# Hash attention and a gated block on one core: weight pieces rounded a row later, with three staging buffers, and the late pairs' sums and hash products put between rows

## The chip, the core and the metric

The kernel runs on one core of a Trainium2 chip. The metric is the device time of one execution in microseconds. A profiled execution gives, besides its time, the span from its first to its last instruction and the granted clock of TensorE. The engines are called PE (TensorE: matmuls), PEld (PE's weight loads), DVE (VectorE), ACT (ScalarE), POOL (GpSimd, which here mainly issues DMAs) and SP (SyncE, which issues DMAs). L146 is line 146 of the kernel before.

## What is computed

The first part is attention in which a query sees only the keys of its own hash bucket; the second is a SwiGLU block on the joined heads.

```python
# q, k, v: (4, 8, 768, 64); proj: (64, 6)
q_bucket = sum((q @ proj > 0) * 2**arange(6))        # k_bucket likewise
scores = where(q_bucket == k_bucket, q @ k.T / 8, -1e9)
attn = exp(scores - max); attn = attn / (sum(attn) + 1e-9)
x = (attn @ v).transpose(0, 2, 1, 3).reshape(3072, 512)
g = x @ w_gate; val = x @ w_val                      # (512, 1536) each
out = (g * sigmoid(g) * val) @ w_out                 # (1536, 512)
```

The three weight matrices come as 64-bit floats, which the kernel reads as pairs of 32-bit words and turns into 32-bit parts itself.

## The kernel before

**Attention.** Two heads of one batch make a pair: 16 pairs, four per batch. A pair has two rows of work, one for each half of its 768 queries (`half` 0 and 1), and a row has six chunks of 128 keys. For each chunk, PE makes the scores of both heads in two PSUM banks: a product of q and k (`sc<-qT,kT`, L428) and, added to it, a product of their hash bits (`sc<-qb,kb`), which decides whether a key is seen. ACT takes the exponentials (`A<-sc`, L431). DVE adds the chunks' exponentials up for the row sums (`acc`, L459 and L463). After the six chunks of a row, PE multiplies the exponentials by v (`av`, L442), and ACT copies the result out (`xT`, L452; `e`, L451). Seven banks serve the scores, the transposes, the hash products (`hps`) and the sums (`sum`); one bank holds `av`.

**Sums.** `total(n)` has PE sum `acc` over the partitions (L474), ACT copy the result to `row` (L477), and SP send it to `few`. `invert` takes reciprocals on DVE (L483), has SP store them and load them back spread over the partitions (L492). `norm` multiplies on DVE (L498). A pair of batch 0 is then split into three parts: ACT rounds it (`high`, L201), and DVE makes the rest (L204, L208). A pair of a later batch is stored to DRAM. Before, `total(n-1)` stands in row (n, 0), after the second chunk; `invert` after that row's scores; `norm` after the scores of row (n, 1).

**The next pair.** `front(n + 1)` gives the steps that make the next pair's `qT`, `kT` and hash bits. The transposes are PE's up to pair 4; from pair 5 on (here the "late" pairs, prepared from pair 4 on) they are DVE's (L396). The last step, `hash_next`, multiplies by the hash directions on PE (L355), takes signs on ACT (L360) and copies q's bits to a second set of partitions with a DMA that SP issues (L372, `qb<-qb`). It stands in row (n, 1) after the third chunk, and the signs of k after the row's last chunk.

**Weight pieces.** The weights are cut into 36 pieces. A piece of words is loaded by POOL (`words`, L116), and `scale` prepares it on ACT with two instructions (L123 into the staging buffer, L124). The generator `prepare` then does the rest in five steps, of which `prepare_on(5)` or `prepare_on(4)` are taken at a row's end, and one after each atom of the gated block:

```python
shift    DVE  L141
or       DVE  L143
add      DVE  L146, then the rounding on ACT  L147, then the load of words 3 pieces on
subtract DVE  L150
low      DVE  L152, then the store of the staging buffer to DRAM by POOL  L154
```

`progress["kept"]` counts the pieces whose store has been issued. `scale_ahead` scales a further piece if it is less than two ahead of `kept`; it is called once or twice between a row's scores and its `av` products, and once after them. There are two staging buffers (`stage`) and four buffers of words. The last pair's result and its spread reciprocals lie in two of the words buffers (`spare`).

**Gated block.** Three parts of x and three of each weight piece give two sums per product, `a` and `n` (L584). Per batch, 12 U items each make a gate and a value (four atoms: 16 matmuls into `a`, 8 into `n`, twice), and 4 D items multiply by `w_out` (six atoms of 9 matmuls, `o`). `a`, `n` and `o` share four buffers of two banks each. ACT evicts `a` (L626), DVE subtracts `n` (L632), ACT takes SiLU (L634), DVE multiplies (L636), ACT rounds (L637), DVE makes the two other parts of `hid` (L640, L642). In the first D of a batch ACT evicts (L671) and DVE subtracts (L676); later DVE does both. `bring` has POOL load the prepared pieces back into a ring of seven buffers (L190), so that a piece has to be stored before it is brought. The order of all engines' queues is the order in which the program text issues the instructions; nothing reorders them.

Of the kernel before, what the change touches and what calls it, by code (L numbers as in the profile page):

```python
# [8 lines left out]
FP32 = mybir.dt.float32  # L9
FP32R = mybir.dt.float32r  # L10
BF16 = mybir.dt.bfloat16
I32 = mybir.dt.int32
# [7 lines left out]
def kernel(  # L20
# [43 lines left out]
    TOWARD = 1 - 2.0**-13  # L64

    konst = ctx.enter_context(tc.tile_pool(name="konst", bufs=1))
    wordp = ctx.enter_context(tc.tile_pool(name="wordp", bufs=4))
    stagep = ctx.enter_context(tc.tile_pool(name="stagep", bufs=2))
    small = ctx.enter_context(tc.tile_pool(name="small", bufs=2))
    even_x = ctx.enter_context(tc.tile_pool(name="even_x", bufs=1))  # L70
    ringp = ctx.enter_context(tc.tile_pool(name="ringp", bufs=7))
    dram = ctx.enter_context(tc.tile_pool(name="dram", bufs=1, space=bass.MemoryType.DRAM))
    ctx.enter_context(tc.manual_schedule())
# [3 lines left out]
    def r32(t):  # L77
        return t.bitcast(FP32R)

    def finish(todo):  # L80
        while todo:
            todo.pop(0)()
# [35 lines left out]
    def scale(i):  # L118
# [5 lines left out]
        nc.scalar.activation(t[:, :, 0], top, AF.Copy, scale=2.0**-13 * (1 + 2.0**-17))  # L124
        progress["scaled"] = i + 1

    def scale_ahead():
        i = progress["scaled"]
        if i < NPIECE and i < progress["kept"] + 2 and i in words:
            scale(i)  # L130

    def prepare():
        for i in range(NPIECE):
            load_words(i + 1)
            if i not in staged:
                scale(i)
            t, st = words[i], staged[i]
            lo, hi = t[:, :, 0], t[:, :, 1]
            w = st[:, 1]
            wi = w.bitcast(I32)  # L140
            nc.vector.tensor_single_scalar(wi, wi, 3, op=ALU.logical_shift_left)  # L141
            yield True
            nc.vector.scalar_tensor_tensor(out=wi, in0=hi, scalar=-(1 << 31), in1=wi,  # L143
                                           op0=ALU.bitwise_and, op1=ALU.bitwise_or)
            yield True
            nc.vector.tensor_tensor(wi, wi, lo, op=ALU.add)  # L146
            nc.scalar.activation(r32(st[:, 0]), w, AF.Copy, scale=TOWARD)  # L147
            load_words(i + 4)
            yield True
            nc.vector.tensor_tensor(r32(w), w, st[:, 0], op=ALU.subtract)  # L150
            yield True
            nc.vector.scalar_tensor_tensor(out=r32(st[:, 2]), in0=w, scalar=-STEP, in1=st[:, 0],  # L152
                                           op0=ALU.mult, op1=ALU.add)
            nc.gpsimd.dma_start(ram[i].bitcast(FP32), st)  # L154
            progress["kept"] = i + 1
            yield True

    preparing = prepare()

# [54 lines left out]
    def attention(scope):  # L214
# [113 lines left out]
        load_words(2, nc.sync)  # L328
        for name, queue in (("q", nc.sync), ("k", nc.gpsimd), ("v", nc.sync)):
            fetch(1, name, queue)  # L330
        load_words(4)

        T = {}
        bits = {}
# [74 lines left out]
        acc = {}  # L409
        av = {}  # L410
        xT = {}
        mean = {}
        waiting = []

# [19 lines left out]
        def attend(u):  # L434
            n, half, c = units[u]
            a = weights(u)
            if c == 0:
                av[n] = av_ps.tile([P, 512], FP32, tag="av", name="av")
            ps = av[n]
            width = AW if half == 0 else HQ  # L440
            for h in range(2):
                nc.tensor.matmul(ps[h * D : (h + 1) * D, 0:width], raws["v", n][:, h, c, :],  # L442
                                 a[:, h, 0:width], start=c == 0, stop=c == NCH - 1)
            if c == NCH - 1:
                if half == 0:
                    if n == len(pairs) - 1:
                        xT[n] = spare()
                    else:
                        xT[n] = xp.tile([P, S], FP32, tag="xT", name="xT")
                    mean[n] = small.tile([P, 1], FP32, tag="e", name="e")  # L450
                    nc.scalar.activation(mean[n], ps[:, HQ : HQ + 1], AF.Copy, scale=EPS)  # L451
                nc.scalar.copy(xT[n][:, half * HQ : (half + 1) * HQ], ps[:, 0:HQ])  # L452
# [29 lines left out]
        def invert(n, few):  # L482
            nc.vector.reciprocal(few, few)  # L483
            s = sums[n % 2]
            nc.sync.dma_start(s, few)
            if n == len(pairs) - 1:
                t = spare().rearrange("p (x q) -> p x q", x=2)
            else:
                t = att.tile([P, 2, HQ], FP32, tag="r", name="r")
            flat = s.rearrange("p e -> (p e)").rearrange("(h x t) -> h (x t)", h=2, t=HQ)  # L490
            for h in range(2):
                nc.sync.dma_start(t[h * D : (h + 1) * D].rearrange("p x t -> p (x t)"),  # L492
                                  flat[h : h + 1].to_broadcast([D, 2 * HQ]))
            return lambda: norm(n, t)
# [15 lines left out]
        def prepare_pair(count):  # L510
            for _ in range(count):
                if steps:
                    rest.extend(f for f in steps.pop(0)() or [] if f)
# [5 lines left out]
        for u in range(0, N, NCH):  # L519
            n, half, _ = units[u]  # L520
            more = n + 1 < len(pairs)
            for c in range(NCH):
                score(u + c)
                if u + c == 2 or more and half == 1 and c == 2:
                    prepare_pair(1)
                if half == 1 and c == 2:
                    load(n + 2, "qk")
                if c == 1 and half == 0 and n > 0:
                    total(n - 1)
                if c:  # L530
                    add(u + c)
            finish(rest)
            if half == 0 and more:
                steps = front(n + 1)
                if u:
                    prepare_pair(2)
            if half == 0:
                while waiting:
                    last.append(waiting.pop(0)())
            else:  # L540
                finish(last)
            for _ in range(1 if u else 2):
                scale_ahead()
            for c in range(NCH):
# [12 lines left out]

    left = []

    def spare():  # L560
        t = wordp.tile([P, PIECE, 2], I32, tag="words", name="words")
        return t.rearrange("p f w -> p (f w)")[:, 0:S].bitcast(FP32)

    with ExitStack() as scope:
        attention(scope)

    def gated_block(scope):
        xs = [even_x, scope.enter_context(tc.tile_pool(name="odd_x", bufs=1))]  # L570
        hidp = scope.enter_context(tc.tile_pool(name="hidp", bufs=4))
        gatep = scope.enter_context(tc.tile_pool(name="gatep", bufs=2))
        outp = scope.enter_context(tc.tile_pool(name="outp", bufs=1))
# [120 lines left out]
        for kind, n in order:  # L694
            if kind == "U":
                b, f = divmod(n, NF)
                if f == NF - NQ and b + 1 < B:
                    for pr in range(NP):
                        x = spare()
                        nc.sync.dma_start(x, kept_x[b + 1, pr])  # L700
                        splits += split(x, b + 1, pr, xs[(b + 1) % 2])
            if kind == "D" and n == B * NF // NQ - 1:
                finish(tails)
            for atom in atoms_of(kind, n):
# [7 lines left out]
                if left and count[0] in (6, 14):  # L712
                    left.append(left.pop(0)())
                    left[:] = [f for f in left if f]
                prepare_on(1)

    with ExitStack() as scope:
        gated_block(scope)
# [32 lines left out]
```

## Time and profile before

| | |
|---|---|
| median of 8 runs | 990.69 us (988.74 to 995.2) |
| the profiled execution | 989.59 us |
| its span | 987.7 us |
| granted TensorE clock, mean | 0.989 |
| PE busy | 953.2 us (97%) |
| DVE busy | 674.8 us (68%) |
| ACT busy | 471.5 us (48%) |
| POOL busy | 124.7 us (13%) |
| first gated matmul (`a`) | at 382.16 us |

The attention part lasts until about 382 us. The first gated batch, with the last pieces of weights, runs until about 490 us; after that PE hardly stands. A line of a list of waits reads: who waited, for whom, total us, how often, longest. In the order of time a line reads: start, duration, engine, line, operation, out<-in, count, and in brackets the idle time before it and what ended it.

### The profile page before, as it was taken

The page shows a single profiled execution, that of the slowest core. Times are in us where ns is not written, and L with a number is a line of the kernel's source. Part 1 is how long each engine was busy: PE and PEld are TensorE (multiplying, and loading weights), DVE is VectorE, ACT ScalarE, POOL GpSimd, SP SyncE. Part 2 cuts the span into 40 slices and gives each one's busy share as a digit, 9 for nine tenths or more (in the row PEclk, how much of TensorE's full clock was granted, in tenths as well). Part 3 has the DMA queues.
Part 4 walks back from the last instruction along what each step waited for, and adds up shares of the span by engine and source line. Part 5 has one row for each costly group of instructions (what it writes and reads, how often), then busy time and mean ns, then how long its engine had stood idle before and what let it go on. Part 6 is the DMA issues. An engine that isn't in the chain of part 4 may idle for free.

```text
span 987.7 us, 14470 instructions
## 1 busy us (share of the span) xinstructions
PE 953.2 (97%) x5413; PEld 729.7 (74%) x5413; DVE 674.8 (68%) x868; ACT 471.5 (48%) x882; POOL 124.7 (13%) x248
## 2 busy tenths in 40 slices
PE   9988899999999999999999999999999999999998
PEld 4444444444444447989999999999999999999996
DVE  4667788778878786868886446586546586546556
ACT  6877776867767675444422332322332322232221
POOL 3110011100101012221210110110110110110100
PEclk9999999999999999999999999999999999999999
DMA  6554575776868867598955854655854655754641
GB/s 181 176 158 136 154 174 145 205 182 185 207 162 205 245 236 262 174 370 346 352 194 177 329 188 144 235 192 184 323 189 156 227 188 192 255 190 162 224 160 64
DMA packets 134262, 203.22 MB, mean 206 GB/s; under 512 B 92912, under 2 KB 98512, under 8 KB 134192
## 3 DMA queue, kind: packets, MB, share of 16 engines
q0 software_dynamic: 31008, 159.79, 45.3%
q1 hardware_dynamic: 102384, 42.30, 17.3%
q8 instruction: 43, 0.70, 0.3%
q10 hardware_dynamic: 800, 0.20, 0.1%
q14 instruction: 27, 0.22, 0.1%
HBM read 162.01 MB, written 39.42 MB: 204 GB/s over the span
## 4 chain that ended last, share of the span: by engine, by line
PE 58%; DVE 1%; issue 1%; DMA 0%; ACT 0%; POOL 0%; POOLq 0%; DVEq 0%; ACTq 0%
PE a L584 27%; PE o L584 18%; PE n L584 13%; DVE o L676 0%; DVE o L673 0%; DMA ram<-stage 0%; ACT stage L123 0%; DVE words L498 0%; DVE hid L640 0%; DVE g L632 0%; DVE stage L143 0%; ACT words L124 0%; POOL words L116 0%; ACT o L671 0%; DVE stage L141 0%
## 5 line engine op out<-in xcount | busy, mean ns | idle before, releaser
L584 PE MATMUL a<-xparts,ring 128*128 128x384 f32 x1536 | 282.7, 335 | 1.9 <-ACT row L477 1.9
L584 PEld LDWEIGHTS a<-xparts,ring 128*128 128x128 f32 x1536 | 268.9, 188 | 3.9 <-ACT row L477 2.6
L584 PE MATMUL o<-ring,hid 128*128 128x512 f32 x864 | 200.4, 391 | 2.2 <-DVE o L676 2.2
L428 PE MATMUL sc<-qT,kT 64*128 64x384 f32 x768 | 176.7, 520 | 20.0 <-ACT A L431 19.8
L584 PEld LDWEIGHTS o<-ring,hid 128*128 128x128 f32 x864 | 162.4, 188 | 35.9 <-DVE o L676 2.7
L431 ACT ACTIVATE A<-sc 128x384 f32<-128x384 f32 x384 | 156.4, 507 | 8.2 <-PE sc L428 7.5
L428 PEld LDWEIGHTS sc<-qT,kT 64*128 64x128 f32 x768 | 84.0, 193 | 90.0 <-issue 46.7
L584 PE MATMUL n<-xparts,ring 128*128 128x384 f32 x768 | 148.5, 334 | 0.0
L463 DVE TENSOR_TENSOR acc<-acc,A 128x768 f32<-128x768 f32 x128 | 122.7, 958 | 25.5 <-ACT A L431 14.4
L584 PEld LDWEIGHTS n<-xparts,ring 128*128 128x128 f32 x768 | 134.5, 188 | 0.0
L442 PE MATMUL av<-A,vraw 128*64 128x386 f32 (+1 forms) x768 | 131.2, 491 | 0.0
L190 POOL DMA_DIRECT2D ring<-ram x144 | 75.9, 529 | 432.9 <-PE n L584 278.1
L632 DVE TENSOR_TENSOR v<-v,n 128x768 f32<-128x768 f32 x48 | 45.8, 954 | 106.0 <-PE n L584 105.4
L442 PEld LDWEIGHTS av<-A,vraw 128*64 128x64 f32 x768 | 52.3, 136 | 71.9 <-issue 57.9
L626 ACT ACTIVATE g<-a 128x768 f32<-128x768 f32 x48 | 38.9, 811 | 125.8 <-PE a L584 122.6
L637 ACT ACTIVATE hid<-v 128x768 fp32r<-128x768 f32 x48 | 40.7, 848 | 118.4 <-DVE v L636 118.4
L428 PE MATMUL sc<-qb,kb 64*128 64x384 bf16 x384 | 82.9, 331 | 3.9 <-DMA qb<-qb 3.3
L634 ACT ACTIVATE g<-g 128x768 f32<-128x768 f32 x48 | 40.6, 847 | 89.2 <-DVE g L632 89.2
L676 DVE TENSOR_TENSOR o<-o 128x512 f32<-128x512 f32 x96 | 65.9, 687 | 22.1 <-ACT o L671 19.6
L632 DVE TENSOR_TENSOR g<-g,n 128x768 f32<-128x768 f32 x48 | 45.6, 950 | 33.4 <-PE n L584 33.3
L154 POOL DMA_DIRECT2D ram<-stage x36 | 19.4, 540 | 360.5 <-issue 139.9
L640 DVE SCALAR_TENSOR_TENSOR hid<-hid,v 128x768 fp32r<-128x768 f32 x48 | 45.9, 957 | 26.3 <-ACT hid L637 26.3
(77 smaller groups left out, 714.9 us busy)
## 6 DMA issues: line engine op xcount, KB each, us to landing
ring<-ram POOLq DMA_DIRECT2D x144, 768.0 KB, 5.8
ram<-stage POOLq DMA_DIRECT2D x36, 768.0 KB, 5.1
vraw<-in_v_dram SPq DMA_DIRECT2D x16, 384.0 KB
words<-in_moe_w_out_dram POOLq DMA_DIRECT2D x12, 512.0 KB, 7.7
out_dram<-o SPq DMA_DIRECT2D x24, 256.0 KB
r<-sums SPq DMA_DIRECT2D x30, 192.0 KB
words<-in_moe_w_gate_dram POOLq DMA_DIRECT2D x11, 512.0 KB, 6.8
words<-in_moe_w_val_dram POOLq DMA_DIRECT2D x11, 512.0 KB, 7.8
```

The lines of the kernel that those rows point to most:

```text
L190: nc.gpsimd.dma_start(t.bitcast(FP32), ram[at].bitcast(FP32))
L428: nc.tensor.matmul(sc[h], x["k", n][rows, ks], x["q", n][rows, qs], start=start, stop=not start)
L431: nc.scalar.activation(weights(u)[:, h, 0:HQ], sc[h], AF.Exp, scale=SCALE * (OFF / 2 if n <= NP else 1.0))
L442: nc.tensor.matmul(ps[h * D : (h + 1) * D, 0:width], raws["v", n][:, h, c, :], a[:, h, 0:width], start=c == 0, stop=c == NCH - 1)
L463: nc.vector.tensor_tensor(acc[n, half], acc[n, half], a[:, :, 0:HQ], op=ALU.add)
L584: nc.tensor.matmul(ps, w, x, start=start, stop=stop)
L626: nc.scalar.activation(two(z), ops[what][2], AF.Copy, scale=STEP + 1)
L632: nc.vector.tensor_tensor(two(z), two(z), n_, op=ALU.subtract)
L634: nc.scalar.activation(z, z, AF.Silu)
L637: nc.scalar.activation(h, val, AF.Copy, scale=TOWARD / STEP)
L640: nc.vector.scalar_tensor_tensor(out=l, in0=h.bitcast(FP32), scalar=-STEP, in1=val, op0=ALU.mult, op1=ALU.add)
L676: nc.vector.tensor_tensor(accs[c], accs[c], t[:, 1], op=ALU.subtract)
```

## The change

The generator `prepare` now works on two pieces at a time: it shifts, combines and adds piece i, and then subtracts and finishes piece i - 1. The rounding is no longer issued with the addition; the piece is put on a list, and `scale_ahead` issues the rounding at its next call, before it looks whether it may scale. A piece may be scaled if it is less than three ahead of `kept`. There are three staging buffers and three buffers of words. `scale_ahead` is also called after every atom of the gated block.

`total(n-1)` moves to the start of row (n, 1), `invert` to after that row's scores, and `norm` to after the scores of row (n+1, 0); the last pair keeps the old places. From pair 4 on, the hash products stand ahead of the scores of half 1, and the signs of k after its second chunk. The last pair's result and reciprocals get a buffer of their own, which later holds parts of x (`odd_x`); the loads of x for the next batch use the three words buffers, after all pieces have been prepared.

```diff
-    wordp = ctx.enter_context(tc.tile_pool(name="wordp", bufs=4))
-    stagep = ctx.enter_context(tc.tile_pool(name="stagep", bufs=2))
+    wordp = ctx.enter_context(tc.tile_pool(name="wordp", bufs=3))
+    stagep = ctx.enter_context(tc.tile_pool(name="stagep", bufs=3))
+    odd_x = {NP - 1: ctx.enter_context(tc.tile_pool(name="odd_x", bufs=1))}
...
+    unrounded = []
+
+    def round_up():
+        st = staged[unrounded.pop(0)]
+        nc.scalar.activation(r32(st[:, 0]), st[:, 1], AF.Copy, scale=TOWARD)
+
     def scale_ahead():
+        if unrounded:
+            round_up()
         i = progress["scaled"]
-        if i < NPIECE and i < progress["kept"] + 2 and i in words:
+        if i < NPIECE and i < progress["kept"] + 3 and i in words:
             scale(i)
 
     def prepare():
-        for i in range(NPIECE):
...
-            nc.vector.tensor_tensor(wi, wi, lo, op=ALU.add)
-            nc.scalar.activation(r32(st[:, 0]), w, AF.Copy, scale=TOWARD)
-            load_words(i + 4)
...
+        for i in range(NPIECE + 1):
+            if i < NPIECE:
...
+                nc.vector.tensor_tensor(wi, wi, lo, op=ALU.add)
+                unrounded.append(i)
+                load_words(i + 3)
+                yield True
+            if i > 0:
+                while i - 1 in unrounded:
+                    round_up()
+                st = staged[i - 1]
+                w = st[:, 1]
+                nc.vector.tensor_tensor(r32(w), w, st[:, 0], op=ALU.subtract)
+                yield True
+                nc.vector.scalar_tensor_tensor(out=r32(st[:, 2]), in0=w, scalar=-STEP,
+                                               in1=st[:, 0], op0=ALU.mult, op1=ALU.add)
+                nc.gpsimd.dma_start(ram[i - 1].bitcast(FP32), st)
+                progress["kept"] = i
+                yield True
...
+            final = not more
+            late = n + 1 > NP
+            if half == 1 and n > 0 and not final:
+                total(n - 1)
+            if half == 1 and more and late:
+                prepare_pair(1)
             for c in range(NCH):
                 score(u + c)
-                if u + c == 2 or more and half == 1 and c == 2:
+                if u + c == 2 or more and half == 1 and c == 2 and not late:
                     prepare_pair(1)
+                if half == 1 and c == 1 and late:
+                    finish(rest)
...
-                if c == 1 and half == 0 and n > 0:
+                if c == 1 and half == 0 and final:
                     total(n - 1)
...
+            if half == 1:
+                finish(last)
+            while waiting and (half == 1 or final):
+                last.append(waiting.pop(0)())
             if half == 0:
-                while waiting:
-                    last.append(waiting.pop(0)())
-            else:
-                finish(last)
+                finish(last[:-1] if final else last)
+                last[:] = last[-1:] if final else []
...
                 if f == NF - NQ and b + 1 < B:
+                    while next(preparing, None):
+                        pass
...
                 prepare_on(1)
+                scale_ahead()
```

## The prediction

> **What bounds the kernel now.** I read the windows by stage first, then who waited for whom, then the order of time at one PE stall, and last the DMA issues. The windows give, for 0 to 382 us (attention), 382 to 490 (first gated batch, in which the last weight pieces are prepared) and the rest: PE busy, PEld, DVE, ACT, POOL, granted clock, DMA share, GB/s.
>
> ```profile
> 0.00:382.00 382.00, 354.82 (x2245) 166.69 (x2245) 288.69 (x388) 277.48 (x628) 42.66 (x94) 0.98 0.68 185
> 382.00:490.00 108.00, 105.61 (x564) 100.66 (x565) 80.95 (x112) 48.02 (x71) 22.57 (x42) 0.98 0.83 307
> 490.00:988.00 498.00, 492.76 (x2605) 462.36 (x2604) 305.17 (x370) 145.98 (x185) 59.52 (x113) 1.00 0.55 199
> ```
>
> PE is the bound everywhere; the time that can be won is its idle time and its slow clock. The waits name both:
>
> ```profile
> ACT stage L147 <- DVE stage L146: 55.1, 25, 9.3
> PE sc L428 <- ACT A L431: 19.8, 11, 3.3
> ACT stage L123 <- DMA ram<-stage: 14.1, 9, 4.1
> PE sc L428 <- DMA qb<-qb: 3.3, 4, 1.7
> PE o L584 <- DVE o L676: 2.2, 1, 2.2
> ```
>
> In order of time, at one of the three longest stalls:
>
> ```profile
> 58.38 0.69 DVE L146 CUSTOM_DVE_ANT_0 stage<-words,stage 128x1024 uint16<-128x1024 uint16 x1
> 59.10 0.63 ACT L147 ACTIVATE stage<-stage 128x512 fp32r<-128x512 f32 x1 [3.60 <-DVE stage L146]
> 59.64 1.61 ACT L431 ACTIVATE A<-sc 128x384 f32<-128x384 f32 x4
> 60.16 1.39 PE L428 MATMUL sc<-qT,kT 64*128 64x384 f32 x3 [3.33 <-ACT A L431]
> ```
>
> ACT stands at the rounding (L147) until DVE's addition (L146) is done, the exponentials queue behind it, no score bank comes free, PE idles 3.33 us. Afterwards the clock is halved for some 3.4 us:
>
> ```profile
> 60.20:64.00 3.80, 3.80 (x15) 3.13 (x17) 2.42 (x3) 3.07 (x9) 0.00 (x0) 0.55 0.64 191
> ```
>
> so (1 - 0.55) x 3.8 = 1.7 us more. Five such stretches follow stalls in attention (60, 88, 115, 204, 330 us): 8.5 us. With 19.8 + 3.3 = 23.1 us of idling, attention has **31.6 us** to give.
>
> The opposite fact is in the gated part: a scaling (L123) that waits for the store of its staging buffer. Here the store was issued by POOL at 417.46, ACT stood 4.78 us, and PE lost 2.23 us in the D product plus a half-clock stretch (again 1.7).
>
> ```profile
> 417.46 0.54 POOL L154 DMA_DIRECT2D ram<-stage  x1
> 425.71 0.66 ACT L123 ACTIVATE stage<-words 128x512 f32<-128x512 f32 x1 [4.78 <-issue]
> 428.19 3.36 PE L584 MATMUL o<-ring,hid 128*128 128x512 f32 x9 [2.23 <-DVE o L676]
> ```
>
> **What the Trainium skill says.** "PSUM — Partial Sum Buffer", section "Engine vs sequencer instructions": the queues of ACT and DVE are strict FIFO. The trace agrees (exponentials behind L147). "TensorE: Matmul & The Clock Gate", Part 1: after an idle window of about 3.4 us the array runs at half clock until it has been busy for about as long. The trace agrees on the length (3.4 us), but a gap of 1.74 us at 203.7 was enough. "DMA: Bandwidth & Descriptors", "Anatomy of one DMA": about 2.0 us + bytes / 436e3; for 128 x 1536 x 4 = 786,432 bytes, 3.8 us. The trace's median for this store is longer:
>
> ```profile
> ram<-stage POOLq DMA_DIRECT2D x36, 768.0 KB, 5.1
> ```
>
> In 380 to 490 us, where DMAs are busier, issues on staging buffers took 4.2 to 14.9 us, median 5.9. I take 5.5.
>
> **The change, part by part.** No arithmetic is added; the built orders have as many rows on PE and DVE.
>
> (a) *Rounding a row later (attention).* It now stands after a row's exponentials, for an addition made a row before: no wait there. The cover is the row itself, some 11 us.
>
> (b) *Sums and hash of late pairs.* Sum products move ahead of the scores of half 1; from pair 4 on the hash products too, and q's copy by DMA on SP gets a whole row: the 3.3 us and the stretch at 204 go. SP's order becomes row sums, q copy, next q/k loads: none waits long. Each late half 1 starts with row (0.49) and two signs (0.57 each), 1.6 us before its first exponential; PE's sum and hash products (0.8 each) cover it. The last pair keeps the old places.
>
> (c) *What remains in attention.* Pairs 1 to 3: ACT's work per pair is 24 exponentials 9.8, k and q copies 1.9, signs 3.6, split 0.84, rounding 1.26, scaling 2.7, rest 1.8: about 22 us, against 22.4 for PE (27.4 between the stalls at 60 and 87, less 3.33 and 1.7). ACT must also wait for DVE's normalisation (L498) before the split's L201: two stalls of about 1.4. In pairs 4 and 5 that wait is long, since DVE's two transposes (0.97 + 0.94) come first. From PE's end of scores s: exponentials end s+1.1 (my estimate: two exponentials of 0.41 and a lag); DVE adds 0.96, transposes, normalises 1.01: s+5.0; ACT split 0.84, rounding 0.63, scaling 1.35, copies 0.65, row 0.49: s+9.0. PE meanwhile does attends 4.1, sum and hash 1.6, two chunks 1.6, has filled seven banks at s+7.3 and waits 1.7 for the sum's bank, then twice about 0.8 for first exponentials and for the hash bank: 3.3, and 4.6 in the row that starts with more backlog. Left: 2.8 + 7.9, plus two half-clock stretches 3.4: 14. Gain 31.6 - 14 = **17.5**; bounds 10 (also other rows stall) and 31.6 (nothing left). The wait between the stages (1.9) loses about 1: the rounding no longer stands ahead of the last row copy.
>
> (d) *Gated part: scaling ahead of need.* Before, a piece is scaled one step after the last piece's store began, into the other buffer. Now scaling follows `kept` directly: each store frees the allowance, and the next instruction on ACT is the scaling into the buffer that the store still reads. Seven scalings after the first stand so. Behind each on ACT: evictions (0.81), SiLU, rounding of h (0.85 each); who waits: PE, for its four pairs of banks (8.3 us of U work, 2.05 us per D chunk). Third staging buffer or not, the awaited store is the newest. I followed the queues by hand from PE's first product (T = 0), with PE 2.77 / 1.39 per a / n block, DVE 0.95, 0.69, the store 5.1 after its issue:
>
> | scaling in | store issued | scaled | PE held: piece, us |
> |---|---|---|---|
> | U0 | 12.5 | 19.0 | U2 a 2.9 |
> | U2 | 27.7 | 34.2 | U3 v 3.5 |
> | U3 | 43.8 | 50.3 | D0 chunk 2 6.9, chunk 5 2.5 |
> | D0 | 61.8 | 68.3 | U4 n 5.1 |
> | U4 | 75.9 | 82.3 | U5 v 3.9 |
> | U5 | 90.8 | 97.3 | D1 3.3 + 0.9 |
> | D1 | 106.5 | 113.4 | D1 last 1.6 |
>
> For instance U0: v's eviction is done at 9.9, DVE subtracts, multiplies, ends the piece at 12.5; the store lands at 17.6, ACT scales to 19.0, evicts U1's first block at 19.8, PE wanted its banks at 16.9. A store comes every 15 us, where PE's five atoms take 10.4. Sum 30.6; with 5.5 instead of 5.1, six times 0.4 more: 33. Bounds: 25 (4.2 each) and 45 (7.2). Taken off: the 2.23 + 1.7 at 428, which is one of these waits already: **+29**. Half clock after them is mostly swallowed by the next wait: 1, bounds 0 and 6.
>
> (e) *Buffers.* Three word buffers for four; the last pair's result no longer sits in two of them, so POOL's 16.3 us wait (words L116 for L498) goes; words issued now land before the store that the same scaling awaits: nothing. x parts of later batches: the fourth load waits for one split, 3 atoms of 18 in hand: nothing; without that cover, SP's output stores would wait some 6 us, which PE sees only at the end.
>
> Sum: -17.5 - 1 + 29 + 1 = **+11.5** on the profiled 989.59 (span 987.7 and 1.9 around it): 1001. The profiled execution lies 1.1 under the median 990.69, less than the steps are known to.
>
> **The rivals.** *Faster:* the store wait stays beside other work, as in 435 to 490 us before, where ACT stood 3.58 us for words (at 435.8) and PE lost nothing; then the gated part costs little (5) and attention gives 25: about 970. For it: ACT is busy 48 of 108 us there. Against: the event at 428. It decides below about 2.6 us lost per scaling (18.5 / 7). *No change:* both cancel, 987 to 993. *Not what it says:* the rounding's wait is replaced in attention too, by scaling standing for the store (14.1 us in 9 before); then attention gives 5 and the time is about 1014. For: same order of store and scaling; against: those waits lie mostly in attends, 6 us after the store.
>
> **How the numbers follow.** Forecast as worked out 0.60, its own range 993 to 1013; stood-for-store in attention 0.08; faster 0.22; cancelled 0.10. Range 970 to 1014, leaving out the ends of the outer cases. 0.3% (3 us) is about what a measurement here tells from no change. Faster 0.22, same 0.10, slower 0.68.
>
> **What would show it.** Right: rounding without waits in attention, sc waiting for A under 10 us, no wait for q's copy; in 360 to 470 us ACT's scaling standing 4 to 7 us for ram<-stage seven times, PE waiting for g, v evictions and o. Wrong: attention ends before 355 or after 372 us by the start of the first a block, or the gated batch loses under 15 us.

## The result and the profile after

The changed kernel takes **1021.11 us** (median of 11 runs, 1017.63 to 1023.8), beside 990.43 for the kernel before on the same chip: ratio 1.030, 95% interval 1.028 to 1.032. The prediction was 1001, range 970 to 1014: the direction was right, the size was not, and the time lies 7 us outside the range. The direction was right through the gated part alone; for attention a gain was forecast and a loss was measured. The span of the profiled execution is 1016.6 us, 28.9 more than before.

The end of attention is taken, as in the prediction, at the start of the first `a` product. It moved from 382.16 to 386.38: **4.2 us later, where 18.5 earlier were predicted** (17.5, and 1 between the stages). From there to the end of the span it was 605.5 us before and is 630.2 now: 24.7 more, where 30 were predicted. The windows by stage, after (columns as before: PE busy, PEld, DVE, ACT, POOL, clock, DMA share, GB/s):

```profile
0.00:386.38 386.38, 361.90 (x2246) 169.93 (x2246) 286.17 (x386) 275.79 (x627) 41.49 (x92) 0.97 0.69 180
386.38:494.38 108.00, 89.84 (x430) 83.00 (x431) 59.57 (x82) 38.74 (x57) 18.62 (x33) 0.89 0.67 239
494.38:1016.60 522.22, 517.10 (x2739) 485.75 (x2738) 326.67 (x401) 155.77 (x198) 64.80 (x123) 1.00 0.57 207
```

In the first gated batch PE stands for 108 - 89.84 = 18.2 us, and the clock of 0.89 takes (1 - 0.89) x 89.84 = 9.9 us more. The waits, after, from the lists for ACT, PE and DVE of the whole span:

```profile
ACT stage L124 <- DMA ram<-stage: 40.7, 11, 7.8
ACT e L467 <- DVE xT L514: 37.2, 7, 7.3
ACT xparts L215 <- DVE xT L514: 17.2, 4, 5.5
ACT e L467 <- PE hps L369: 11.6, 3, 4.2
ACT stage L132 <- DVE stage L155: 9.6, 4, 3.2
PE sc L443 <- ACT row L493: 13.7, 8, 5.4
PE sc L443 <- ACT A L446: 4.3, 8, 1.0
DVE xT L514 <- DMA r<-sums: 21.5, 8, 6.7
```

(L124 is L123 of before, the scaling; L132 is L147, the rounding; L155 is L146, the addition; L467 is L451, the mean `e`; L514 is L498, the normalisation; L215 is L201, the split; L493 is L477, the row copy; L501 and L508 are L485 and L492, the store of the reciprocals and their spread copy `r`; L268 loads q and k of late pairs; L369 is L355, the hash products; L410 is L396, DVE's transposes; L443 and L446 are L428 and L431, the scores and exponentials; L499 is L483, the reciprocals; L168 is L154, the store of a piece; L607 is L584, the gated products; L649 is L626, the eviction of `a`.) The rounding's 55.1 us are down to 9.6, all four of them in the gated part. PE's waits for exponentials fell from 19.8 to 4.3 us. In their place stands a wait that was not in the kernel before: **ACT stands at the mean `e` for DVE's normalisation**, and PE stands behind the row copy that follows it. It is larger than the 37.2 us of the list. The three waits of 11.6 us that the list puts down to the hash products are the same wait: the mean does not read these products, all ten waits end 0.09 to 0.10 us after a normalisation has ended, and a third buffer for the mean (below) ends them all. Together they are 48.8 us.

PE's idle time alone does not show the loss: in attention it is 386.38 - 361.90 = 24.5 us, less than the 382 - 354.82 = 27.2 before. What grew is PE's busy time, by 7.1 us for the same products. About 2 us of it are a slower clock (estimated by adding (1 - clock) x busy time over stretches of 4 us, which gives 7.6 us before and 9.7 after). The other 5 were not traced.

The longest such stall in order of time, with the four engines that make it:

```profile
326.63 6.86 SPq L268 DMA_DIRECT2D qraw<-in_q_dram  x4
333.54 4.54 SPq L268 DMA_DIRECT2D kraw<-in_k_dram  x4
334.74 0.22 DVE L499 RECIPROCAL few<-few 128x12 f32<-128x12 f32 x1
338.18 0.59 SPq L501 DMA_DIRECT2D sums<-few  x1
344.43 1.13 SPq L508 DMA_DIRECT2D r<-sums  x2
351.77 1.02 DVE L514 SCALAR_TENSOR_TENSOR xT<-xT,e,r 128x768 f32<-128x768 f32 x1 [6.70 <-DMA r<-sums]
352.88 0.17 ACT L467 ACTIVATE e<-av 128x1 f32<-128x1 f32 x1 [7.28 <-DVE xT L514]
353.31 0.50 ACT L493 COPY row<-sum 128x384 f32<-128x384 f32 x1
353.86 1.00 PE L443 MATMUL sc<-qT,kT 64*128 64x384 f32 x1 [5.43 <-ACT row L493]
```

The reciprocals are ready at 334.96. SP issues eight loads of q and k ahead of them, so their store goes out at 338.18, the spread copy `r` at 344.43; DVE stands for it until 351.77. So of 16.8 us from the reciprocals to the normalisation only 3.2 are spent until the store is issued; 6.3 pass until `r` can be issued, and 7.3 more until DVE starts. In the kernel before, `r` was issued 1.4 to 3.1 us after the store throughout attention. The mean `e` of pair n+1 is a tile of the pool `small`, which has two buffers; its buffer is the one of pair n-1, which the normalisation has yet to read. So ACT, which has only a 128 x 1 copy to make, waits for DVE, and with it the row copy, the signs and the next exponentials. The first score product after the stall takes 1.00 us, where one alone took 0.48 at 330.64: the clock is halved.

In the gated part, a scaling that stands for the newest store, at D0:

```profile
431.19 0.54 POOL L168 DMA_DIRECT2D ram<-stage  x1 [7.99 <-issue]
435.43 0.66 ACT L124 ACTIVATE stage<-words 128x512 f32<-128x512 f32 x1 [5.42 <-DMA ram<-stage]
436.53 0.79 ACT L649 ACTIVATE v<-a 128x768 f32<-128x768 f32 x1
437.37 11.11 PE L607 MATMUL o<-ring,hid 128*128 128x512 f32 x36 [5.87 <-ACT v L649]
```

This is what the prediction drew; the store landed sooner than it took (the DMA issues of 386 to 490 us give a median of 4.2 us for it, beside the 5.5 assumed).

### The profile page after: what moved, and what is told of

Read it like the earlier page. It is cut to its first block, busy times and chain, and to the rows that moved or that the text cites. A ratio compares the mean times of both kernels' runs of the same rounds, so it can differ in the third digit from the quotient of the medians.

```text
span 1016.6 us, 14489 instructions
## 1 busy us (share of the span) xinstructions
PE 968.8 (95%) x5413; PEld 738.7 (73%) x5413; DVE 672.4 (66%) x868; ACT 470.3 (46%) x882; POOL 124.9 (12%) x248
## 3 DMA queue, kind: packets, MB, share of 16 engines
q1 hardware_dynamic: 102384, 42.30, 17.5%
## 4 chain that ended last, share of the span: by engine, by line
PE 50%; issue 5%; DMA 3%; DVE 2%; ACT 1%; ACTq 0%; POOLq 0%
PE a L607 22%; PE o L607 17%; PE n L607 11%; DMA ram<-stage 3%; DVE o L699 1%; DVE o L696 0%; ACT words L125 0%; DVE v L655 0%; ACT v L649 0%; ACT stage L124 0%; ACT stage L132 0%; ACT L657 0%; ACT g L649 0%; DVE v L659 0%; DVE hid L665 0%
## 5 line engine op out<-in xcount | busy, mean ns | idle before, releaser
L607 PE MATMUL a<-xparts,ring 128*128 128x384 f32 x1536 | 285.6, 337 | 5.6 <-ACT g L649 4.0
L607 PEld LDWEIGHTS a<-xparts,ring 128*128 128x128 f32 x1536 | 271.2, 190 | 8.2 <-ACT g L649 4.3
L607 PE MATMUL o<-ring,hid 128*128 128x512 f32 x864 | 204.1, 396 | 9.4 <-ACT v L649 5.9
L443 PE MATMUL sc<-qT,kT 64*128 64x384 f32 x768 | 186.2, 520 | 20.3 <-ACT row L493 13.7
L607 PEld LDWEIGHTS o<-ring,hid 128*128 128x128 f32 x864 | 164.7, 191 | 44.9 <-ACT v L649 6.3
L446 ACT ACTIVATE A<-sc 128x384 f32<-128x384 f32 x384 | 154.8, 511 | 8.4 <-PE sc L443 7.7
L607 PE MATMUL n<-xparts,ring 128*128 128x384 f32 x768 | 149.9, 336 | 4.5 <-DVE o L699 4.5
L443 PEld LDWEIGHTS sc<-qT,kT 64*128 64x128 f32 x768 | 84.8, 195 | 89.8 <-issue 43.3
L607 PEld LDWEIGHTS n<-xparts,ring 128*128 128x128 f32 x768 | 135.6, 189 | 4.8 <-DVE o L699 4.8
L479 DVE TENSOR_TENSOR acc<-acc,A 128x768 f32<-128x768 f32 x128 | 122.7, 959 | 17.2 <-ACT A L446 4.6
L649 ACT ACTIVATE g<-a 128x768 f32<-128x768 f32 x48 | 38.9, 810 | 126.7 <-PE a L607 123.0
L443 PE MATMUL sc<-qb,kb 64*128 64x384 bf16 x384 | 81.7, 333 | 0.9 <-DVE kb L383 0.5
L168 POOL DMA_DIRECT2D ram<-stage x36 | 19.7, 547 | 408.7 <-ACT A L446 173.2
```

Of the source, the lines that this page charges most:

```text
L443: nc.tensor.matmul(sc[h], x["k", n][rows, ks], x["q", n][rows, qs], start=start, stop=not start)
L446: nc.scalar.activation(weights(u)[:, h, 0:HQ], sc[h], AF.Exp, scale=SCALE * (OFF / 2 if n <= NP else 1.0))
L479: nc.vector.tensor_tensor(acc[n, half], acc[n, half], a[:, :, 0:HQ], op=ALU.add)
L607: nc.tensor.matmul(ps, w, x, start=start, stop=stop)
L649: nc.scalar.activation(two(z), ops[what][2], AF.Copy, scale=STEP + 1)
```

## The experiments

Each compares with runs of the kernel before on the same chip. "End" is the end of attention in the trace, "rest" the span from there on; the ratio is to the kernel before, with its 95% interval. "Part one" is the weight pipeline with its buffers, "part two" the new main loop of attention (sums, hash products and normalisation in their new places); the "gated call" is the new call of `scale_ahead` after every atom of the gated block.

| kernel | end | rest | median us | ratio |
|---|---|---|---|---|
| before | 382.2 | 605.5 | 990 to 992 | 1 |
| after | 386.4 | 630.2 | 1021.1 | 1.030 (1.028 to 1.032) |
| three turns for the mean | 377.6 | 627.9 | 1012.2 | 1.023 (1.019 to 1.027) |
| sums before loads | 474.0 | 629.4 | 1104.7 | 1.114 (1.111 to 1.118) |
| no gated call | 389.4 | 601.6 | 992.7 | 1.001 (1.000 to 1.003) |
| part one alone | 359.6 | 629.1 | 990.5 | 1.000 (0.998 to 1.001) |
| part two alone | 398.7 | 607.2 | 1006.8 | 1.017 (1.015 to 1.019) |
| normalisation later | 367.9 | 628.6 | 997.5 | 1.008 (1.005 to 1.010) |
| gated call, older store | 387.6 | 601.5 | 992.7 | 1.002 (1.000 to 1.003) |
| part one, no gated call | 358.7 | 601.7 | 961.7 | 0.971 (0.968 to 0.973) |
| sums on POOL | 384.4 | 632.0 | 1014.4 | 1.024 (1.019 to 1.028) |
| three turns, sums on POOL | 378.7 | 631.8 | 1012.8 | 1.022 (1.017 to 1.027) |
| part one, no call, ring later | 359.9 | 608.5 | 968.5 | 0.977 (0.973 to 0.981) |
| sums early only, no call | 352.6 | 601.6 | 956.9 | 0.965 (0.960 to 0.970) |

The column "rest" has three levels: 601.5 to 601.7 without the wait for the newest store, 605.5 to 607.2 with the old weight preparation, 628 to 632 with the gated call. One run, with the ring later, lies between. So the two losses can be taken apart. Each end and each rest comes from one profiled execution: three kernels with the same attention (after, no gated call, older store) end it at 386.4, 389.4 and 387.6, so a difference of less than about 3 us in the column "end" says nothing.

**The mean's buffer.**

```diff
-                    mean[n] = small.tile([P, 1], FP32, tag="e", name="e")
+                    mean[n] = small.tile([P, 1], FP32, tag="e", name="e", bufs=3)
```

> Edit: the buffer for the key mean (tag e) has three turns instead of two, nothing else, on the changed kernel. Theory A (ScalarE stands at the mean of pair n+1 because its buffer is read by the normalisation of pair n-1, which the change moved to the end of that row): ScalarE's 37.2 us of waiting at L467 for L514 fall below 5, the six PE stalls behind the row copy from 165 us on go with their half-clock stretches, attention ends 12 to 20 us earlier than 386 (the stalls of the first pairs at 91, 117 and 141 stay, since the split waits for the same normalisation there): 1001 to 1009 us. Theory B (VectorE is late itself, since the reciprocals' broadcast r comes behind the q and k loads on the SP queue): the wait moves to the spread of k's signs, which stands behind the normalisation on VectorE, PE then waits for kb; attention ends within 6 us of before: 1014 to 1021.

Attention ended 8.7 us earlier, and ACT's wait at the mean for the normalisation was gone, and so were the three listed for the hash products. That is less than the 12 of theory A and more than the 6 of theory B. Where the rest went, from the lists of PE and DVE:

```profile
PE hps L369 <- DVE qT L410: 12.3, 7, 5.7
...
DVE xT L514 <- DMA r<-sums: 24.1, 11, 5.0
```

DVE still stands for `r`, as theory B had said; PE no longer waits for the row copy of late pairs but for DVE's transposes at the hash products, which neither theory had named.

**The reciprocals ahead of the loads.**

```diff
-                if half == 1 and c == 2:
-                    load(n + 2, "qk")
...
             while waiting and (half == 1 or final):
                 last.append(waiting.pop(0)())
+            if half == 1:
+                load(n + 2, "qk")
```

> Edit: in half 1 the loads of q and k of the pair after next are issued behind the sums' store and the broadcast r on SP, as the kernel before had it, nothing else. Theory B (r is late because eight loads of 0.7 to 1.7 us each are issued ahead of it): VectorE's 21.5 us of waiting for r at L514 fall below 3, ScalarE's waits at L467 fall from 37.2 to 15 to 22 us (what is left is VectorE's additions and transposes ahead of the normalisation), attention ends 6 to 12 us earlier: 1009 to 1015. Theory A alone (only the additions and transposes hold the normalisation): the waits at L467 stay above 30 us, time 1018 to 1023. A price to look for: the transposes of the next pair may wait for the later loads.

It was far off: 84 us slower than the changed kernel. DVE no longer waits for `r`, and ACT stands at the mean for the normalisation not less but more, 95.3 us: the price that the expectation mentioned in its last sentence is everything, since the transposes now wait for k, and the normalisation stands behind them on DVE. From DVE's and PE's lists:

```profile
DVE kT L410 <- DMA kraw<-in_k_dram: 82.6, 11, 11.3
...
PE hps L369 <- DVE qT L410: 84.0, 11, 11.5
```

In the changed kernel a late pair's hash products stand half a row earlier than before, so q and k are wanted earlier too; in the two orders tried, SP brings either the reciprocals or q and k late. This run does not price `r`'s lateness.

**The gated call left out.**

```diff
                 prepare_on(1)
-                scale_ahead()
```

> Edit: the call that scales a piece ahead in the gated part is left out (one line); the roundings there are then issued when the subtraction asks for them. Theory (the scaling stands for the store of the buffer it will overwrite, and that is the newest one): PE idle from 386 us on falls from 18.3 to under 6 us and the clock there returns to about 0.98 from 0.89; time 997 to 1003. Rival 1 (the wait is for words, with three buffers in place of four, or for the rounding): idle stays above 12, time 1012 to 1020. Rival 2 (the addition and the rounding now stand close together in that part, as in attention before): ScalarE waits at L132 for L155, and half of the gain is given back: 1005 to 1011.

PE's idle time in the first gated batch is nil and the clock full, from the windows by stage:

```profile
389.37:497.37 108.00, 108.00 (x588) 103.46 (x589) 83.63 (x116) 49.82 (x73) 24.32 (x44) 1.00 0.84 311
```

The median fell by 1021.1 - 992.7 = 28.4 us, all of it in the rest, and lies below the range expected. The rest is also 3.9 us shorter than before the change, which is the size of the stall at 428 us that the prediction took off. Rival 2 did not come: ACT has no wait for the addition in this run.

**Part one alone** (the main loop of attention as before; the weight pipeline, its buffers and the gated call as after).

> Edit: the changed kernel with the main loop of attention as it was before (sums, hash products and normalisation in their old places); the two-piece weight pipeline, three staging and three word buffers, and the gated call stay. Theory (the loss in attention comes from the second part, the gain from the first): attention ends 12 to 20 us before 382, with no wait of ScalarE at the mean for the normalisation; the gated part is as slow as in the changed kernel (25 us over before): 995 to 1003 us. Rival (the loss comes from the new weight order itself: scaling or rounding in ScalarE's queue meets the store): attention still ends after 380 us, time 1013 to 1022.

Attention ends 22.5 us earlier than before, so part one's gain was real and part two took it away. The gain is 2.5 us over the range expected, and the time below it.

**Part two alone** (only the main loop of attention as after).

> Edit: the kernel before with only the main loop of attention of the changed kernel (sums ahead of half 1, hash products of late pairs in it, normalisation at the end of the next half 0); weight preparation, buffers and gated part as before. Theory (it is this new order that costs attention 27 us, by making ScalarE stand for a normalisation that comes a half pair earlier): ScalarE waits 15 us or more at the mean and the split for the normalisation and VectorE waits for r over 10 us, on top of the 55 us at the rounding; attention ends after 390 us, gated part as before (605.6): 1000 to 1020 us. Rival (the new order costs only together with the weight pipeline, since the rounding's wait before left room for r): attention ends at 376 to 386 us, time 984 to 994.

Attention ends 16.5 us later than before, and the time is in the theory's range. ACT waits 17.7 us at the split for the normalisation. At the mean it waits 24.0 us, which the list puts down to the hash products; here too each wait ends 0.09 to 0.10 us after a normalisation has ended:

```profile
ACT e L451 <- PE hps L355: 24.0, 8, 4.9
...
291.16 0.98 DVE L498 SCALAR_TENSOR_TENSOR xT<-xT,e,r 128x768 f32<-128x768 f32 x1
291.65 0.49 PE L355 MATMUL hps<-kT,hash 128*32 128x384 f32 x2
292.23 0.17 ACT L451 ACTIVATE e<-av 128x1 f32<-128x1 f32 x1 [4.92 <-PE hps L355]
```

In this run the hash products end at the same moment in all eight waits, so it cannot tell the two apart by itself; the changed kernel, with two buffers and with three, does. So ACT's part of the theory holds (at the rounding it waits 43.6 us besides), and DVE's does not: it waits for `r` only once, 2.9 us. The normalisation holds the mean up even where `r` is in time, because it stands behind five additions and two transposes on DVE (from 284.28 to 291.16 in the row shown). The two parts alone would give 22.5 - 16.5 = 6.0 us of gain in attention, and together they lose 4.2: about 10 us come only from their meeting. How the 16.5 divide between these waits and PE's was not followed further.

**The normalisation half a pair later** (with three turns for the mean).

```diff
-            if half == 0:
-                finish(last[:-1] if final else last)
-                last[:] = last[-1:] if final else []
+            if half == 0 and final:
+                finish(last[:-1])
+                last[:] = last[-1:]
```

> Edit: the changed kernel with three turns for the key mean and with the normalisation (and the split behind it) issued at the end of half 1 of the next pair, half a pair later; sums and hash products stay in their new places, and the gated call stays. Theory (the early place of the normalisation is the whole loss of the second part): ScalarE's waits at the mean and the split for it (37.2 + 17.2 us) and VectorE's wait for r (21.5) fall below 4 each, PE's stalls behind the row copy go, attention ends at 356 to 364 us: 991 to 999 us. Rival (the hash products half a row earlier need q and k sooner than SP brings them): PE waits for the transposes (hps for qT), over 10 us, and attention ends at 368 to 378: 1003 to 1013.

Attention ends at 367.9, 18.5 us earlier than in the changed kernel; both `r` and the mean no longer hold anything up, and the split's 17.2 us are 7.5. Of the 18.5, a third buffer alone had given 8.7; the other 9.8 are the later place. So the early place of the normalisation, with two buffers for the mean, is the largest part of part two's loss, 18.5 of 26.8 us, but not the whole. The time, 997.5, is in the theory's range; for what is left the rival had the right wait:

```profile
PE hps L369 <- DVE qT L410: 13.2, 11, 2.5
```

**The gated call, with the store one older.**

```diff
-    def scale_ahead():
+    def scale_ahead(ahead=3):
...
-        if i < NPIECE and i < progress["kept"] + 3 and i in words:
+        if i < NPIECE and i < progress["kept"] + ahead and i in words:
...
-                scale_ahead()
+                scale_ahead(2)
```

> Edit: the changed kernel, with the gated call kept but allowed to scale a piece only when the store of its staging buffer is not the newest one but one older (2 in place of 3 ahead of the stores in that one call). Theory (only the wait for the newest store costs): ScalarE's 40.7 us of waiting for ram<-stage fall below 8, PE idle from attention's end on below 6 us, 990 to 997 us, as with the call left out (992.7) or a little less. Rival (what costs is ScalarE work put between the evictions there, wherever its store stands): PE idle there stays above 10 us, time 1003 to 1015.

As without the call: 992.7 us, ACT's wait for `ram<-stage` 5.2 us, and PE does not stand in the gated batch. So it is not ACT's work there that costs, but the scaling's wait for a store issued just before.

**Part one without the gated call.**

> Edit: the weight pipeline alone with its three buffers (main loop of attention as before), and without the call in the gated part. Theory (gain in attention and loss in the gated part are independent): attention ends at 358 to 362 us as with the pipeline alone (359.6), and the rest takes 603 to 607 us: 962 to 970 us, faster than both kernels. Rival (what attention gains is given back, since the weight pieces and the ring are then late for the gated part): PE waits there for ring or for additions, 975 to 988 us.

961.7 us, just below what was expected: gain and loss are independent, and the kernel is 2.9% faster than the kernel before.

**The reciprocals on POOL's queue.**

```diff
-            nc.sync.dma_start(s, few)
+            nc.gpsimd.dma_start(s, few)
...
-                nc.sync.dma_start(t[h * D : (h + 1) * D].rearrange("p x t -> p (x t)"),
+                nc.gpsimd.dma_start(t[h * D : (h + 1) * D].rearrange("p x t -> p (x t)"),
```

> Edit: the changed kernel with the store of the reciprocals and the broadcast r issued by POOL in place of SP, at the same place of the program; the loads of q and k keep their place on SP. Theory (r is late because SP issues eight loads of q and k ahead of it): VectorE's 21.5 us of waiting for r at L514 fall below 6, ScalarE's waits for the normalisation (37.2 at the mean, 17.2 at the split) to 30 to 40 together, and attention ends 4 to 10 us ahead of 386: 1011 to 1017 us. Rival (the additions and transposes ahead of the normalisation on VectorE hold it anyway): ScalarE's waits stay above 48 together, attention ends within 3 us of 386: 1018 to 1023.

The time is in the theory's range, the end is not. DVE's wait for `r` is nil, and ACT's at the mean falls to two of 8.5 us together (listed, as above, for the hash products; each ends 0.09 us after a normalisation): at 345.32 the normalisation follows the transposes at once, where it came 6.7 us after them in the changed kernel. On POOL's queue the store of the reciprocals and `r` took 3.2 and 3.4 us to land (medians of 150 to 380 us), with the loads of q and k still on SP's; which suggests that `r` was late for standing behind these loads on one queue, more than for the traffic as such. Yet attention ends only 2.0 us earlier, which is no difference here. ACT's and POOL's waits within attention say why:

```profile
ACT stage L124 <- DMA ram<-stage: 33.3, 7, 7.3
...
POOL sums L501 <- DVE few L499: 116.5, 10, 20.8
```

POOL now stands for the reciprocals, its weight store comes late behind them, and ACT's scaling stands for that store (4.3 us in attention in the changed kernel). One wait was exchanged for another. Since ACT stands at that scaling ahead of the mean, the run doesn't tell how long it would have stood at the mean itself.

**Three turns for the mean, and the reciprocals on POOL.**

> Edit: as the one before (reciprocals and r on POOL), and three turns for the key mean. Theory (two causes of the stalls: the mean's buffer, and r late on VectorE): attention ends 6 to 12 us earlier than with three turns alone (377.6), at 366 to 372, with the early pairs' split as what is left: 995 to 1001 us. Rival (once ScalarE need not wait for the mean, r's lateness lies beside other work): attention ends at 375 to 379: 1003 to 1008.

Attention ends at 378.7, the rival's figure, though the time, 1012.8, is above both ranges. But the scaling's wait (26.8 us in attention) confounds this run like the last, so it does not show that a late `r` is harmless once the mean has three turns. What it would be worth to have `r` early at no price stays open.

**The ring two rows later** (part one without the gated call, and ring loads from `N - 5 * NCH` in place of `N - 7 * NCH`).

> Edit: the weight pipeline alone without the gated call (961.7 us), and the first ring loads start five rows before the end of attention in place of seven. Theory (the one wait of VectorE for k, 9.5 us at 317 to 326, comes from two ring loads, a store and a words load that share the DMA engines with SP's eight loads, whose issue takes 21 us there against 5.5 elsewhere): that wait falls below 2 us, PE's 7.9 us for qT go with their half clock, attention ends at 347 to 352: 950 to 956 us. Rival (the same collision comes two rows later, or the gated part then waits for ring): 958 to 966 us.

A miss, worse than the rival: 968.5 us. The wait for k stayed where it was, until 327 us, and is 7.6 us, and PE stood 3.7 us in the gated part for a piece not ready.

**The sums early, and nothing else of part two** (the normalisation later, with its three turns for the mean, with `late = False`, and without the gated call).

> Edit: as the run with the normalisation later (three turns for the mean, normalisation at the end of half 1; attention ended at 367.9), and in addition the hash products and signs of the late pairs back in their old place within the scores of half 1, so that of the second part only the earlier sum products are left; the gated call is left out. Theory (the 8 us by which 367.9 is over the 359.6 of the pipeline alone are the late pairs' hash products, which follow VectorE's transposes too closely: 13.2 us of PE waiting at hps for qT): that wait falls below 8, attention ends at 356 to 362, the rest takes 601 to 603: 958 to 965 us, no better than the 961.7 of the pipeline alone without the call. Rival (the earlier sum products are the price): attention ends at 366 to 370, 968 to 973 us.

Better than expected: attention ends at 352.6, 7.0 us earlier than with part one alone, and PE's wait for the transposes is down to one of 4.1 us. The median is 956.9, the fastest kernel here, 3.5% faster than the kernel before; its interval overlaps that of part one alone by a little, so that its lead over it rests on the trace.

## Why the prediction was wrong, and where it was right

The sum was -17.5 - 1 + 29 + 1 = +11.5. Measured from the same ends: attention +4.2 instead of -18.5, the rest +24.7 instead of +30. The first error is 22.7 us upward, the second 5.3 downward; 11.5 + 22.7 - 5.3 is the 28.9 of the span.

**(a) Rounding a row later: right.** It has no wait left in attention. With part one alone, attention gains 22.5 us, more than the 17.5 that was forecast for the whole.

**(b) A step that failed too, at a price that stays open: "SP's order becomes row sums, q copy, next q/k loads: none waits long."** The list left out that the store of the reciprocals and `r` are now issued behind those loads, because the inversion moved to the end of half 1 and the loads stayed after its third chunk. Before, the inversion was half a pair away from them, and DVE waited for `r` 0.6 us in all; after, 21.5. The steps of (c) timed the normalisation from DVE's own queue alone, at about four microseconds after the scores; at the longest stall it came 11 us after them. But part two alone stalls at the mean with `r` in time, and the runs that brought `r` early either held up q and k or the weight store, so how much of the loss is `r`'s is not shown.

**(c) The failed step: what remains in attention, "Left: 2.8 + 7.9", which puts the pairs after 5 at nothing.** The prediction saw ACT wait for the normalisation only at the split, hence for pairs of batch 0. It did not follow the mean's two buffers: before, the normalisation was issued a row ahead of the buffer's next writer; now it is issued in that writer's own row, just ahead of it. So the wait comes in every pair from 6 on, split or not: ten times, 48.8 us. From 160 us on PE stands 14.5 us in attention and loses about 5 more to the half clock (estimated from the same stretches of 4 us), where the sum had nothing (its worst case for other rows still left a gain of 10). In the early pairs, where the prediction did expect stalls, it was not too low: PE stands 5.3 us behind the splits, where 10.7 were expected for pairs 1 to 5. A third buffer for the mean gives back 8.7 us, and with a later normalisation 18.5.

The runs give the account of attention in one chain, each step from the row of the table before it: the weight pipeline -22.5 (382.2 to 359.6, part one alone), the sums' products ahead of half 1, with the normalisation at the end of a half 1, -7.0 (to 352.6), the late pairs' hash products ahead of the scores +15.3 (to 367.9, with the gated call, which comes after attention), the mean's buffer and the early normalisation +18.5 (to 386.4), of which a third mean buffer alone gives back 8.7. The sizes hold for this order of the steps, as the two parts are not additive, and each to about 3 us. Of the 15.3, PE's waits for the transposes explain 13.2 - 4.1 = 9.1; the rest was not traced. The prediction had counted the early hash products as a gain (q's copy, 3.3 us and a half-clock stretch; that wait is indeed down to 0.3).

**(d) The gated part: right mechanism, two terms mis-sized.** Scalings stand for the newest store, evictions behind them, PE behind those; the call left out and the call with an older store both give it all back. PE's holds were put at 33 us and measured 18.2, with stores of 4.2 in place of 5.5 and five holds in place of nine. The half clock was put at 1, "mostly swallowed by the next wait", with 6 as bound, and measured 9.9: PE ran 8 us or more from each hold to the next, longer than a slow stretch of some 3.4 us lasts, so little was swallowed. Together 28.1 against 34. The prediction's test for this part named seven stands of 4 to 7 us; the trace has seven between 390 and 481 us, of 2.5 to 7.8. The 3.9 us taken off for the stall at 428 agree with what the rest gains over the kernel before once the call is left out.

**(e) Buffers: right.** Neither three word buffers nor the new home of the last pair's result shows in the rest, which is 601.6 without the call.

**The rivals.** "Stays beside other work" named what decides, the loss per scaling, with a bound of 2.6 us; it came to 28.1 / 7 = 4.0, so this rival fell. "Rounding's wait replaced in attention too" is the nearest: a wait of ACT took the place of the rounding's, but for DVE and not for the store, which cost 4.3 us there. It had a chance of 0.08, and its 1014 was the range's end. The prediction's own test (attention ending before 355 or after 372) told the failure.

## What to carry to other kernels

When a step is moved, follow the last reader and the next writer of each small tile that it touches, and count every DMA that now stands ahead of its own on the queue. A lookahead that is freed by an event should not wait for that same event: allowing the scaling only when the store is one older gave back 28 us. The parts of a change are worth separating before they are judged: here the pipeline without the gated call was 2.9% faster, and of the second part's three moves only the earlier sum products were worth keeping, with a third buffer for the mean and a later normalisation.

## What the runs showed of the hardware that was not expected

**Issuing a load is not of fixed price.** Four loads of q or k took SP 2.75 and 2.76 us to issue in the changed kernel at 235 and 238 us, where POOL had no transfer under way; here, in part one without the gated call, while POOL had a weight store, words and two ring loads under way:

```profile
303.50 9.45 SPq L268 DMA_DIRECT2D qraw<-in_q_dram  x4
312.99 11.54 SPq L268 DMA_DIRECT2D kraw<-in_k_dram  x4
```

What stands behind such loads on the queue is late by that much. Which of POOL's transfers lengthens the issue was not isolated; moving the ring loads by two rows left the wait at 7.6 us.

**Gaps well below 3.4 us can be followed by the half clock, and the length of one gap does not decide it.** Hash products after two gaps, with the normalisation later, and then the scores at a stall of the changed kernel with its clock (the last but two of the columns):

```profile
137.03 0.70 PE L369 MATMUL hps<-qT,hash 128*32 128x384 f32 x2 [2.54 <-DVE qT L410]
...
162.55 0.52 PE L369 MATMUL hps<-qT,hash 128*32 128x384 f32 x2 [1.80 <-DVE qT L410]
```

```profile
233.45 0.59 PE L443 MATMUL sc<-qT,kT 64*128 64x384 f32 x1 [0.94 <-ACT row L493]
234.99 2.03 PE L443 MATMUL sc<-qT,kT 64*128 64x384 f32 x4 [0.47 <-ACT A L446]
235.00:238.00 3.00, 3.00 (x10) 2.34 (x12) 0.66 (x2) 2.94 (x7) 0.00 (x0) 0.50 0.48 83
```

After 2.54 us the products slowed (the next pair took 0.86), after 1.80 they did not (0.52 and 0.49), while the kernel before had a slow stretch behind a gap of 1.74, and in the changed kernel two gaps of 0.94 and 0.47 close together came before a clock of 0.50. The Trainium skill, "TensorE: Matmul & The Clock Gate", Part 1, gives an idle window of about 3.4 us; here the measurement decides: the half clock followed shorter gaps, and what decides besides the length of one gap was not tried.
